# Value loads in 128 rows, first-layer weights in long rows, zero products as TensorE filler, three sigmoids in one operation

## The chip, the cores and the metric

The kernel runs on one core of one Trainium2 chip. That core has five engines, each with its own queue that it works off in order: TensorE (PE in the profile; its weight loads are listed apart as PEld), VectorE (DVE), ScalarE (ACT), GpSimd (POOL) and SyncE (SP), which here only issues transfers. Sixteen DMA engines move data between HBM and the on-chip memory SBUF. TensorE writes its sums to PSUM. The metric is the device time of one execution in microseconds (us); lower is better.

## What is computed

An attention layer with a narrow local window and block summaries, then a gated feed-forward layer:

```
B, H, S, D = 4, 8, 768, 64           # block 32, window 16
k_sum = max of k over each block;  v_sum = mean of v over each block
scores_l = scale * q @ k.T,  kept where |i - j| < 16
scores_s = scale * q @ k_sum.T + log(32)
a = softmax([scores_l, scores_s]);   x = a @ [v, v_sum]        # heads joined: (B, S, 512)
x_prev = x shifted by one token
xk = mu_k * x + (1 - mu_k) * x_prev;   xr = mu_r * x + (1 - mu_r) * x_prev
k = relu(xk @ w_k) ** 2              # w_k 512 x 1024
out = sigmoid(xr @ w_r) * (k @ w_v)  # w_r 512 x 512, w_v 1024 x 512
```

The three weight matrices arrive as 64-bit floats. The kernel loads both 32-bit words of each number and joins them into a 32-bit float on the chip.

## The kernel before, in words

The work is cut into eight halves (4 batches x 2 halves of 384 tokens) and, for attention, into four pairs of heads. `load_set(b, p)` loads the keys of a pair (`kt`) and its values in two tiles (`vx`, one for each half); in batch 0 TensorE forms the block means of the values (L405, then L425) and they are spread into the value tiles (L431). `unit(b, p, hf, ...)` is the attention of one pair and half: scores on TensorE (L466), mask on VectorE (L477), exponential on ScalarE (L481), the sum's inverse on VectorE (L487, L488), normalization on GpSimd (L493), transposes on TensorE (L500), copies on ScalarE (L504), the product with the values (L513). In the words below "unit 0'" is the second half's pair 0, "unit 1'" its pair 1, and so on. `mix` makes xk and xr (L535 on ScalarE, L541 on VectorE). The gate is `gate_parts` for the first half (32-bit products of four passes, L580) and `gate_tile` for the others (two-term split products, L567 to L569), each followed by `sigmoid` (L558). `experts` is the feed-forward layer: for each of eight slices j of 128 hidden units the first product (L601), relu and square on ScalarE (L608, L610), the second product (L627). The first half works with the 32-bit weights, the others with split weights made by `split` (L349 or L350, L352).

`weight` loads one 512 KB block of weights into one of three buffers `st` and makes the 32-bit block in four instructions: a scaling (L318 on ScalarE or L321 on GpSimd), and on VectorE L325, L328 and the join L332. There are 4 blocks of w_r and 8 each of w_k and w_v, and each load waits for a buffer that L328 and the scaling of an earlier block have freed.

ScalarE holds one table of functions at a time: the exponential and the sigmoid are in different ones, so each move between L481 and L558 puts an ACT_TABLE_LOAD ahead of the instruction.

The order of everything is set when the program is built. All operations are recorded with a due time, and `Plan.schedule` places them one after another with a table of assumed lengths (`LENGTH`, `DMA_NS_PER_BYTE`); each engine's instructions then stand in that order. Operations named `warm` (L680) are products of the identity matrix with itself, of which no result is used; the plan places one where TensorE has nothing else to start, up to the first gate product, and the rest are dropped.

Of the kernel before, what the change touches and what calls it, by code (L numbers as in the profile page):

```python
# [9 lines left out]
F32 = mybir.dt.float32  # L10
F32R = mybir.dt.float32r
U32 = mybir.dt.uint32
AF = mybir.ActivationFunctionType
ALU = mybir.AluOpType
# [28 lines left out]
    result=695, wbits=340, wor=612, wsub=612, tiny=60,  # L43
    exp=380, pts=380, vm=160, mixa=520, cast=405, relu=525, square=530, sigmoid=500, wscale=570, wcast=530,
# [12 lines left out]
SLACK = 400  # L57
WARM = 150
COLD = 10000
EARLY = 15000  # L60
# [38 lines left out]
class Plan:  # L99
# [36 lines left out]
    def schedule(self):  # L136
# [24 lines left out]
        for o in self.ops:  # L161
            if not waiting[o]:
                released(o)
        spare = [o for o in self.ops if o.name == "warm"]
        while any(ready.values()):
            best = None
            for e, now in engines.items():
                pick = None
                for o, at in ready[e]:
                    start, need, ok = max(at, now, o.due - EARLY if e == "SP" else 0), {}, True  # L170
                    for x in o.bufs:
                        if x.place is None:
# [16 lines left out]
                if pick and (best is None or pick[2] < best[2]):  # L189
                    best = pick + (e,)  # L190
# [29 lines left out]
            order.append(o)  # L220
            if o.name == "gate32" and spare:

                for w in spare:
                    for x in w.bufs:
                        x.left -= 1
                        if not x.left:
                            free_slots[x.pool].append((start, x.place))
                spare = []
                ready["PE"] = [x for x in ready["PE"] if x[0].name != "warm"]
            if o.name == "warm":  # L230
                spare.remove(o)
            for s in o.succ:
# [7 lines left out]
def tile_kernel(ctx: ExitStack, tc: tile.TileContext, q, k, vT, v, mask, ident, pool, sel, mu, w_k, w_v, w_r, out):  # L240
# [35 lines left out]
    sel_sb = const.tile([P, NS], F32, name="sel_sb")  # L276
    MASK, IDENT, MU, OM, POOLM, SEL = [((x, 0),) for x in ("mask", "ident", "mu", "om", "pool", "sel")]

# [22 lines left out]
    def weight(name, i, src, last, due=None):  # L301
        st, we, wc = buf("st"), buf("we"), buf("wc")
        wf = w_f[name, i] = buf("wc") if last else buf("w", F32, False)
        shape = src.shape
        whole = [(wc, 0)]

        def load():
            s = src.bitcast(U32)
            d = st.t.rearrange("p (c a) -> p c a", c=shape[1]) if len(shape) == 3 else st.t
            nc.sync.dma_start(out=d, in_=s)  # L310

        def words():
            w = st.t.rearrange("p (a b) -> p a b", b=2)
            return w[:, :, 1], w[:, :, 0]


        def scale_act():
            nc.scalar.activation(wc.t.bitcast(F32), words()[0].bitcast(F32), AF.Copy, scale=2.0**-112)  # L318
# [12 lines left out]
        def join():
            nc.vector.scalar_tensor_tensor(  # L332
                out=wf.t.bitcast(U32), in0=wc.t, scalar=3, in1=we.t, op0=ALU.logical_shift_left, op1=ALU.bitwise_or)

        op("SP", "load", due, load, writes=[(st, 0)], size=P * 4096)
        op("ACT", "wscale", None, scale_act, reads=[(st, 0)], writes=whole, other=("POOL", "wscale_p", scale_pool))
        op("DVE", "wbits", None, low, reads=[(st, 0)], writes=[(we, 0)])
        op("DVE", "wor", None, sign, reads=[(st, 0), (we, 0)], writes=[(we, 0)])
        op("DVE", "wor", None, join, reads=[(we, 0), *whole], writes=[(wf, 0)])

# [216 lines left out]
    def sigmoid(ps, z):  # L557
        op("ACT", "sigmoid", None, lambda: nc.scalar.activation(z.t, ps.t, AF.Sigmoid), reads=[(ps, 0)], writes=[(z, 0)])  # L558
# [16 lines left out]
    def gate_parts(x, z):  # L575

        ps = [buf("mm") for _ in range(NTT)]
        for p in range(NPAIR):
            for t in range(NTT):
                op("PE", "gate32", GATE0 - (NPAIR - 1 - p) * FIRST + 930 * t, lambda p=p, t=t: nc.tensor.matmul(  # L580
                    ps[t].t, x[p].t[:, t * P:(t + 1) * P], w_f["wr", p].t, start=(p == 0), stop=(p == NPAIR - 1)),
                   reads=[(x[p], 0), (w_f["wr", p], 0), *([(ps[t], 0)] if p else [])], writes=[(ps[t], 0)])
        for t in range(NTT):
            sigmoid(ps[t], z[t])

# [86 lines left out]
    for i in range(NCK):  # L672
        weight("wr", i, w_r[i * P:(i + 1) * P, :], False)
    for j in range(NCV):
        weight("wk", j, w_k[:, j * P:(j + 1) * P].rearrange("(c p) n -> p c n", p=P), False)
        weight("wv", j, w_v[j * P:(j + 1) * P, :], j == NCV - 1)

    spare = buf("mm", F32, False)
    for _ in range(WARM):
        op("PE", "warm", 1.0e8, lambda: nc.tensor.matmul(  # L680
            spare.t[:, 0:P], ident_sb, ident_sb, start=True, stop=True), reads=IDENT, writes=[(spare, 0)])
    sets, gates = [], []
# [120 lines left out]
```

## Time and profile before

| | |
|---|---|
| time, median of 3 runs | 474.1 us (472.27 to 476.43) |
| the profiled execution | 475.29 us, of it 473.5 us from the first to the last instruction (the span) |
| mean granted TensorE clock over the span | 0.993 |
| busy share: PE, DVE, ACT, POOL | 95%, 56%, 62%, 24% |
| DMA: moved, mean rate | 51.16 MB, 108 GB/s |
| the chain that ended last: PE, ACT, DVE, DMA | 67%, 12%, 8%, 8% |

All times in a profile row count from the span's start. A timeline row reads: start, duration, engine, line of the kernel, operation, what it writes and reads, shapes, how many instructions were merged, and in brackets the idle time of the engine before it with what ended that. A 32-bit product appears as two records, so "x8" for L601 is four instructions. A windows row gives for each engine the busy time in that stretch, then the granted clock, the busy share of the DMA engines and their rate in GB/s.

### The profile page before, as it was taken

How to read it: one execution, taken by the hardware profiler on the slowest of the kernel's cores; microseconds unless marked ns; L12 is line 12 of the kernel's file. 1: busy time of each engine (PE TensorE's matmuls, PEld its weight loads, DVE VectorE, ACT ScalarE, POOL GpSimd, SP SyncE). 2: the span in 40 equal slices, each digit the busy share in tenths (PEclk: the TensorE clock that was granted, in tenths of full speed). 3: DMA queues.
4: the chain of work that ended last, by engine and by line, in shares of the span. 5: the costliest groups of instructions: out<-in, count | busy, mean ns of one | idle time of the engine just before them, and what ended most of it. 6: DMA issues, size and time to landing. Idle time of an engine off the chain costs nothing.

```text
span 473.5 us, 9475 instructions
## 1 busy us (share of the span) xinstructions
PE 447.6 (95%) x3438; PEld 357.9 (76%) x3438; DVE 267.0 (56%) x865; ACT 292.6 (62%) x815; POOL 112.5 (24%) x236
## 2 busy tenths in 40 slices
PE   2798799989899999999999999999999999999996
PEld 2664455546688888997778888997778889888995
DVE  3599789989453566527554565529354554222223
ACT  3578987878785756418886756428886655231311
POOL 0453470734133201302442201304242201000000
PEclk9999889999999999999999999999999999999999
DMA  7995368986110209807200219707100010001001
GB/s 245 257 261 158 105 207 262 289 263 148 51 59 12 68 1 304 211 0 228 60 8 9 78 37 301 212 1 219 35 9 9 12 43 26 1 0 68 0 1 66
DMA packets 27013, 51.16 MB, mean 108 GB/s; under 512 B 2903, under 2 KB 14807, under 8 KB 26967
## 3 DMA queue, kind: packets, MB, share of 16 engines
q1 hardware_dynamic: 26967, 50.56, 36.7%
q8 instruction: 27, 0.44, 0.4%
q14 instruction: 19, 0.16, 0.1%
HBM read 42.49 MB, written 6.29 MB: 103 GB/s over the span
## 4 chain that ended last, share of the span: by engine, by line
PE 67%; ACT 12%; DVE 8%; DMA 8%; issue 2%; POOL 1%; SPq 1%; ACTq 0%; POOLq 0%; DVEq 0%
PE mm L627 23%; PE mm L601 22%; ACT y L481 5%; PE pt L500 4%; PE av L513 4%; DMA kt<-in_k 3%; PE mm L567 3%; PE mm L569 3%; PE mm L568 3%; PE sc L466 2%; DMA pool_sb<-in_pool 2%; PE mm L580 2%; ACT L481 2%; DMA st<-in_w_k 1%; POOL y L493 1%
## 5 line engine op out<-in xcount | busy, mean ns | idle before, releaser
L601 PE MATMUL mm<-xs,w 128*128 128x384 f32 x736 | 152.1, 355 | 0.6 <-DVE w L332 0.6
L601 PEld LDWEIGHTS mm<-xs,w 128*128 128x128 f32 x736 | 131.3, 190 | 13.9 <-issue 3.7
L493 POOL TENSOR_SCALAR y<-y,rc 128x120 f32<-128x120 f32 x192 | 93.9, 507 | 156.1 <-DVE rc L488 131.6
L627 PE MATMUL mm<-w,kh 128*128 128x512 f32 x336 | 91.9, 402 | 0.0
L608 ACT ACTIVATE r<-mm 128x384 f32<-128x384 f32 x64 | 31.2, 488 | 93.9 <-PE mm L601 93.8
L481 ACT ACTIVATE y<-y,mn 128x120 f32<-128x120 f32 x192 | 73.5, 386 | 10.7 <-DVE mn L477 10.4
L627 PEld LDWEIGHTS mm<-w,kh 128*128 128x128 f32 x336 | 60.7, 188 | 11.1 <-DVE kl L616 0.2
L614 DVE CAST kh<-r 128x384 fp32r<-128x384 f32 x44 | 15.9, 362 | 74.9 <-ACT r L610 74.8
L477 DVE CUSTOM_DVE_ANT_0 y<-sc,mask_sb 128x120 f32<-128x120 f32 x192 | 42.5, 277 | 22.9 <-PE sc L466 19.6
L627 PE MATMUL mm<-w,kl 128*128 128x512 f32 x168 | 52.4, 407 | 0.1
L549 DVE TENSOR_TENSOR xs<-xa,xs 128x384 fp32r<-128x384 f32 x56 | 30.4, 558 | 23.6 <-ACT xs L547 23.2
L500 PE MATMUL pt<-ident_sb,y 128*120 128x128 f32 x192 | 33.9, 285 | 6.4 <-POOL y L493 6.0
L504 ACT COPY pts<-pt 120x384 f32<-120x384 f32 x64 | 30.3, 473 | 15.6 <-PE pt L500 15.4
L466 PE MATMUL sc<-kt,qt 64*64 64x120 f32 x768 | 30.4, 289 | 8.6 <-DMA pool_sb<-in_pool 6.8
L500 PEld LDWEIGHTS pt<-ident_sb,y 128*120 128x120 f32 x192 | 22.8, 139 | 19.0 <-POOL y L493 9.6
L481 ACT ACTIVATION_READ_ACCUMULATOR y<-y,mn 128x1 f32 x192 | 36.3, 189 | 0.0
L541 DVE SCALAR_TENSOR_TENSOR xa<-vx,mu_sb,xa 128x384 f32<-128x384 f32 x56 | 33.8, 630 | 2.7 <-ACT xa L535 1.8
L627 PEld LDWEIGHTS mm<-w,kl 128*128 128x128 f32 x168 | 30.0, 188 | 6.5 <-DVE kl L616 0.5
L466 PEld LDWEIGHTS sc<-kt,qt 64*64 64x64 f32 x768 | 22.2, 143 | 16.7 <-DVE kt L393 6.8
L567 PE MATMUL mm<-w,xs 128*128 128x512 f32 x84 | 33.6, 400 | 1.1 <-ACT r L608 0.8
L610 ACT ACTIVATE r<-r 128x384 f32<-128x384 f32 x64 | 33.6, 525 | 1.2
L616 DVE TENSOR_TENSOR kl<-r,kh 128x384 fp32r<-128x384 f32 x56 | 31.7, 566 | 4.3 <-ACT kh L615 1.3
(64 smaller groups left out, 548.1 us busy)
## 6 DMA issues: line engine op xcount, KB each, us to landing
vx<-in_v SPq DMA_DIRECT2D x32, 360.0 KB
kt<-in_k SPq DMA_DIRECT2D x15, 544.0 KB
qt<-in_q SPq DMA_DIRECT2D x32, 192.0 KB
out<-z SPq DMA_DIRECT2D x24, 256.0 KB
st<-in_vT SPq DMA_DIRECT2D x12, 384.0 KB
st<-in_w_k SPq DMA_DIRECT2D x8, 512.0 KB
st<-in_w_v SPq DMA_DIRECT2D x8, 512.0 KB
st<-in_w_r SPq DMA_DIRECT2D x4, 512.0 KB
```

What stands on the lines that cost most here:

```text
L466: nc.tensor.matmul(sc[h].t[cs, i, 0:NK], qt.t[hs, n * QW:(n + 1) * QW], kt.t[hs, w * KB:w * KB + NK], start=True, stop=True,)
L477: op("DVE", "mask", None, lambda h=h, i=i, var=var: nc.vector.tensor_tensor_reduce(out=y[h].t[:, i, :], in0=sc[h].t[:, i, 0:NK], in1=mask_ ...
L481: op("ACT", "exp", None, lambda h=h, i=i: nc.scalar.activation(y[h].t[:, i, :], y[h].t[:, i, :], AF.Exp, bias=mn[h].t[:, i:i + 1], scale=-1.0,
L493: op("POOL", "norm", None, lambda h=h, i=i: nc.gpsimd.tensor_scalar(out=y[h].t[:, i, :], in0=y[h].t[:, i, :], scalar1=rc.t[:, NSL * h + i: ...
L500: nc.tensor.transpose(out=pt[h].t[0:NK, i * P:(i + 1) * P], in_=y[h].t[:, i, :], identity=ident_sb)
L541: op("DVE", "mixd", None, lambda: nc.vector.scalar_tensor_tensor(out=xa.t, in0=xt.t[:, 1 + lo:1 + lo + HT], scalar=mu_sb[:, which, p:p + 1 ...
L567: nc.tensor.matmul(ps.t, xh.t[:, ts], h, start=(p == 0), stop=False)
L601: nc.tensor.matmul(ps.t[:, 0:HT], w.t[:, p * P:(p + 1) * P], (x[p] if single else x[p][s]).t, start=(n == 0), stop=(n == len(terms) * NPAI ...
L608: op("ACT", "relu", None, lambda: nc.scalar.activation(r.t, ps.t[:, 0:HT], AF.Relu), reads=[(ps, 0)], writes=[(r, 0)])
L610: op("ACT", "square", None, lambda: nc.scalar.activation(r.t, r.t, AF.Square), reads=[(r, 0)], writes=[(r, 0)])
L616: op("DVE", "sub", None, lambda: nc.vector.tensor_tensor(out=kl.t, in0=r.t, in1=kh.t.bitcast(F32), op=ALU.subtract), reads=[(r, 0), (kh, 0 ...
L627: nc.tensor.matmul(acc[t].t, a.t[:, t * P:(t + 1) * P], v.bitcast(F32) if single else v, start=start, stop=stop)
```

## The change

Four edits, and a new order that follows from them:

1. **Values.** The host pads each value window from 120 rows (96 tokens and 24 summary rows) to 128 with zeros, and a load writes all 128 partitions: 384 KB where it was 360 KB. Rows stay 3072 bytes long.
2. **First-layer weights.** The host stores w_k block by block, so that a load has 128 rows of 4096 bytes; before it had 512 rows of 1024 bytes.
3. **Filler.** A tile of zeros is written by GpSimd at the start; the filler products read it instead of the identity matrix (which had to be loaded), write to unused columns of the transposes' PSUM bank, and may stand anywhere in the first 110 us of the plan, wherever the plan sees TensorE wait over 300 ns. 65 of them end up in the program, 15 before.
4. **Sigmoids of the first gate.** The three are one operation of the plan, so they stand together on ScalarE.

The table's DMA rate goes from 290 to 330 bytes per ns, which with the points above makes the plan order many operations anew.

```diff
+    ..., sigmoid=500, sigmoid3=4000, ...
-DMA_NS_PER_BYTE = 1 / 290.0
+DMA_NS_PER_BYTE = 1 / 330.0
-WARM = 150
-COLD = 10000
+WARM = 260
+WARM_END = 110000
+GAP = 300
+COLD = 5000
...
-                pick = None
+                pick = fill = None
+                if e == "PE" and now > WARM_END:
+                    ready[e] = [x for x in ready[e] if x[0].name != "warm"]
                 for o, at in ready[e]:
+                    if o.name == "warm":
+                        fill = max(now, at), o
+                        continue
...
+                if fill and (pick is None or pick[2] > fill[0] + GAP):
+                    pick = None, fill[1], fill[0]
...
-            if o.name == "gate32" and spare:
-                ...
-                ready["PE"] = [x for x in ready["PE"] if x[0].name != "warm"]
...
             op("SP", "load", None, lambda hf=hf: nc.sync.dma_start(
-                out=windows(vw[hf]), in_=v[b, p, hf]),
-               writes=[(vw[hf], "a"), (vw[hf], "b")], size=NK * HW * 512)
+                out=vw[hf].t[:, 0:S], in_=v[b, p, hf]),
+               writes=[(vw[hf], "a"), (vw[hf], "b")], size=P * HW * 512)
...
-        for t in range(NTT):
-            sigmoid(ps[t], z[t])
+        def sigmoids():
+            for t in range(NTT):
+                nc.scalar.activation(z[t].t, ps[t].t, AF.Sigmoid)
+        op("ACT", "sigmoid3", None, sigmoids, reads=[(a, 0) for a in ps], writes=[(a, 0) for a in z])
...
-        weight("wk", j, w_k[:, j * P:(j + 1) * P].rearrange("(c p) n -> p c n", p=P), False)
+        weight("wk", j, w_k[j], False)
...
-    spare = buf("mm", F32, False)
+    op("POOL", "tiny", -1.0e6, lambda: nc.gpsimd.memset(zero_sb, 0.0), writes=ZERO)
+    spare = pools["pt"][0][:, 512 - P:512]
     for _ in range(WARM):
-        op("PE", "warm", 1.0e8, lambda: nc.tensor.matmul(
-            spare.t[:, 0:P], ident_sb, ident_sb, start=True, stop=True), reads=IDENT, writes=[(spare, 0)])
+        op("PE", "warm", 1.0e8, lambda: nc.tensor.matmul(spare, zero_sb, zero_sb, start=True, stop=True), reads=ZERO)
```

The first place where the order moves is ScalarE between the last mixes of the first half and the exponentials of units 0' (`y_91`, `y_92`) and 1' (`y_93`, `y_94`); `z` are the sigmoids' results, `wc` the scalings of weight blocks, `r` relu and square. Before:

```order
L535 ACTIVATE xs_0_575<-vx_79,om_sb 128x384
L318 ACTIVATE wc_126<-st_122 128x512
L349 CAST w_0_581<-w_0_563 128x512
L558 ACT_TABLE_LOAD
L558 ACTIVATE z_108<-mm_135 128x512
L481 ACT_TABLE_LOAD
L481 ACTIVATE y_91,sm_100<-y_91,mn_95 128x120 x3
L481 ACTIVATE y_92,sm_100<-y_92,mn_96 128x120 x3
L558 ACT_TABLE_LOAD
L558 ACTIVATE z_109<-mm_133 128x512
L558 ACTIVATE z_110<-mm_134 128x512
```

and with the change:

```order
L514 ACTIVATE xs_0_601<-vx_79,om_sb 128x384
L307 ACTIVATE wc_127<-st_124 128x512
L307 ACTIVATE wc_126<-st_122 128x512
L328 CAST w_0_611<-w_0_595 128x512
L460 ACTIVATE y_91,sm_100<-y_91,mn_95 128x120 x3
L460 ACTIVATE y_92,sm_100<-y_92,mn_96 128x120 x3
L565 ACT_TABLE_LOAD
L565 ACTIVATE z_108<-mm_133 128x512
L565 ACTIVATE z_109<-mm_135 128x512
L565 ACTIVATE z_110<-mm_132 128x512
```

The exponentials of unit 0' now stand ahead of all three sigmoids, and one pair of table loads is gone; both versions then go on with relu and square of slice 0, one more table load, and the exponentials of unit 1'.

The second place is TensorE at the same point: from the scores of unit 1' (`kt_62`) to the first product of slice 1, whose weights are `w_0_652` before and `w_0_689` after. The transposes of unit 0' read `y_91` and `y_92`. Before:

```order
L466 MATMUL sc_129<-kt_62,qt_65 64x120 x2
L500 MATMUL pt_130<-ident_sb,y_91 120x128 x3
L466 MATMUL sc_128<-kt_63,qt_66 64x120 x2
...
L601 MATMUL mm_135<-xs_0_565,w_0_652 128x384
...
L500 MATMUL pt_130<-ident_sb,y_92 120x128 x3
```

and with the change:

```order
L445 MATMUL sc_129<-kt_62,qt_65 64x120 x2
L664 MATMUL pt_130<-zero_sb 128x128 x6
L479 MATMUL pt_130<-ident_sb,y_91 120x128 x3
L664 MATMUL pt_130<-zero_sb 128x128 x8
L479 MATMUL pt_130<-ident_sb,y_92 120x128 x3
L584 MATMUL mm_133<-xs_0_578,w_0_689 128x384
```

The scores of unit 2' (`kt_63`), which stood between, have moved behind slice 2, and 14 filler products stand in the place.

The third place is ScalarE at the gate of the second half, whose sigmoids are still three operations (`z_111`, and twice a tile of the last buffer). Before:

```order
L558 ACT_TABLE_LOAD
L558 ACTIVATE z_111<-mm_135 128x512
...
L558 ACTIVATE z_0_1242<-mm_135 128x512
L504 COPY pts_106<-pt_130 120x384
L481 ACT_TABLE_LOAD
L481 ACTIVATE y_93,sm_101<-y_93,mn_97 128x120 x3
L481 ACTIVATE y_94,sm_101<-y_94,mn_98 128x120 x3
L547 CAST xs_0_769<-xa_112 128x384
L558 ACT_TABLE_LOAD
L558 ACTIVATE z_0_1242<-mm_135 128x512
```

and with the change:

```order
L460 ACTIVATE y_93,sm_101<-y_93,mn_97 128x120 x3
L460 ACTIVATE y_94,sm_101<-y_94,mn_98 128x120 x3
L537 ACT_TABLE_LOAD
L537 ACTIVATE z_111<-mm_133 128x512
L505 COPY vx_74<-av_131 128x384
L537 ACTIVATE z_0_1345<-mm_133 128x512
...
L537 ACTIVATE z_0_1345<-mm_133 128x512
```

Here too the exponentials stand ahead of the gate now, and a pair of loads is gone: the whole program has 18 table loads, 22 before.

More of the change, by code (lines that the diff above doesn't have):

```diff
@@ L43 @@
     result=695, wbits=340, wor=612, wsub=612, tiny=60,
-    exp=380, pts=380, vm=160, mixa=520, cast=405, relu=525, square=530, sigmoid=500, wscale=570, wcast=530,
+    exp=380, pts=380, vm=160, mixa=520, cast=405, relu=525, square=530, sigmoid=500, sigmoid3=4000, wscale=570, wcast=530,
     norm=345, wscale_p=640, wcast_p=640, mixa_p=860, kcopy_p=630, evac_a=375, fill=735,
@@ L163, in schedule @@
                 released(o)
-        spare = [o for o in self.ops if o.name == "warm"]
         while any(ready.values()):
@@ L220, in schedule @@
             order.append(o)
-            if o.name == "gate32" and spare:
[L223 to L228, printed above, removed]
-                ready["PE"] = [x for x in ready["PE"] if x[0].name != "warm"]
-            if o.name == "warm":
-                spare.remove(o)
             for s in o.succ:
@@ L276, in tile_kernel @@
     sel_sb = const.tile([P, NS], F32, name="sel_sb")
-    MASK, IDENT, MU, OM, POOLM, SEL = [((x, 0),) for x in ("mask", "ident", "mu", "om", "pool", "sel")]
+    zero_sb = const.tile([P, P], F32, name="zero_sb")
+    MASK, IDENT, MU, OM, POOLM, SEL, ZERO = [((x, 0),) for x in ("mask", "ident", "mu", "om", "pool", "sel", "zero")]
     op("SP", "load", None, lambda: nc.sync.dma_start(out=mask_sb, in_=mask), writes=MASK, size=P * 3 * NK * 4)
@@ L303, in weight @@
         wf = w_f[name, i] = buf("wc") if last else buf("w", F32, False)
[L304 to L318, printed above, removed]
@@ L331, in join @@
[L331 to L338, printed above, removed]
@@ L339, in weight, with words @@
-        op("DVE", "wor", None, join, reads=[(we, 0), *whole], writes=[(wf, 0)])
+        def words(n):
+            return st.t.rearrange("p (a b) -> p a b", b=2)[:, :, n]
+        op("SP", "load", due, lambda: nc.sync.dma_start(out=st.t, in_=src.bitcast(U32)), writes=[(st, 0)], size=P * 4096)
+        op("ACT", "wscale", None, lambda: nc.scalar.activation(
+            wc.t.bitcast(F32), words(1).bitcast(F32), AF.Copy, scale=2.0**-112), reads=[(st, 0)], writes=[(wc, 0)],
+           other=("POOL", "wscale_p", lambda: nc.gpsimd.tensor_scalar(
+               out=wc.t.bitcast(F32), in0=words(1).bitcast(F32), scalar1=2.0**-112, scalar2=1.0, op0=ALU.mult, op1=ALU.mult)))
@@ new lines, in weight @@
+        op("DVE", "wbits", None, lambda: nc.vector.tensor_scalar(
+            out=we.t, in0=words(0), scalar1=29, scalar2=None, op0=ALU.logical_shift_right), reads=[(st, 0)], writes=[(we, 0)])
+        op("DVE", "wor", None, lambda: nc.vector.scalar_tensor_tensor(
+            out=we.t, in0=words(1), scalar=0x80000000, in1=we.t, op0=ALU.bitwise_and, op1=ALU.bitwise_or),
+           reads=[(st, 0), (we, 0)], writes=[(we, 0)])
+        op("DVE", "wor", None, lambda: nc.vector.scalar_tensor_tensor(
+            out=wf.t.bitcast(U32), in0=wc.t, scalar=3, in1=we.t, op0=ALU.logical_shift_left, op1=ALU.bitwise_or),
+           reads=[(we, 0), (wc, 0)], writes=[(wf, 0)])
@@ L737, in feature_major, with words @@
         return a.reshape(B, NPAIR, 2, S, D).transpose(0, 1, 2, 4, 3).reshape(B, NPAIR, P, S)
-    def words(a):
-        return np.ascontiguousarray(a).view(np.int64)
+    def words(a, n):
+        return np.ascontiguousarray(a).reshape(n, P, DM).view(np.int64)
     q, k, v = (np.asarray(inputs[n]) for n in "qkv")
@@ L787 @@
         "mu": mu.reshape(2, NPAIR, P).transpose(2, 0, 1),
-        "w_k": words(inputs["moe_w_k"]),
-        "w_v": words(inputs["moe_w_v"]),
-        "w_r": words(inputs["moe_w_r"]),
+        "w_k": words(np.asarray(inputs["moe_w_k"]).reshape(NCK, P, NCV, P).transpose(2, 1, 0, 3), NCV),
+        "w_v": words(np.asarray(inputs["moe_w_v"]), NCV),
+        "w_r": words(np.asarray(inputs["moe_w_r"]), NCK),
     }
```

16 lines of the change are left out of this document (4 added, 12 removed).

## The prediction

> **What bounds the kernel now.** I read the page's head and slices first, to see which engine is full and when; then the table by stretches; then the order of time on the engines where TensorE has holes.
>
> ```profile
> span 473.5 us, 9475 instructions
> PE 447.6 (95%) x3438; PEld 357.9 (76%) x3438; DVE 267.0 (56%) x865; ACT 292.6 (62%) x815; POOL 112.5 (24%) x236
> PE   2798799989899999999999999999999999999996
> PEclk9999889999999999999999999999999999999999
> ```
>
> One digit is 11.8 us. TensorE is full from the tenth slice on; its holes lie in the first ten, and so does the only dip of its clock. The stretches say the same in numbers (columns: busy us of PE, PEld, DVE, ACT, POOL, then clock, DMA share, GB/s):
>
> ```profile
> 20.00:30.00 10.00, 10.00 (x161) 8.33 (x161) 7.86 (x33) 7.09 (x25) 4.03 (x9) 1.00 1.00 246
> 30.00:40.00 10.00, 10.00 (x75) 4.74 (x73) 9.66 (x17) 7.53 (x21) 7.18 (x8) 1.00 0.70 219
> 50.00:60.00 10.00, 6.56 (x57) 4.09 (x57) 5.94 (x27) 9.90 (x30) 4.83 (x8) 0.75 0.45 134
> 70.00:80.00 10.00, 10.00 (x57) 5.67 (x56) 9.83 (x19) 7.30 (x15) 1.60 (x3) 1.00 0.80 248
> 150.00:200.00 50.00, 50.00 (x328) 43.44 (x329) 29.36 (x82) 29.65 (x73) 9.72 (x23) 1.00 0.49 141
> 400.00:450.00 50.00, 50.00 (x247) 44.55 (x246) 13.89 (x30) 13.61 (x28) 0.00 (x0) 1.00 0.05 17
> ```
>
> From 150 to 200 us and from 400 to 450 TensorE is busy for all 50 us at full clock: nothing in the change shortens that work, so what is won before about 125 us stays won, and nothing else can be. In the early part the bound moves: transfers (share 1.00) until about 30 us, VectorE (9.66 of 10) to 50, ScalarE (9.90) from 50 to 60, VectorE again (9.83) from 70. The stretch from 50 to 60 is the poorest: TensorE works 6.56 of 10 us at three quarters of its clock.
>
> **The sigmoids and the filler, 46 to 66 us.** ScalarE first, then TensorE, then VectorE:
>
> ```profile
> 46.20 0.61 ACT L349 CAST w<-w 128x512 fp32r<-128x512 f32 x1
> 46.83 1.28 ACT L558 ACT_TABLE_LOAD   x1
> 48.12 0.60 ACT L558 ACTIVATE z<-mm 128x512 f32<-128x512 f32 x1
> 48.74 1.28 ACT L481 ACT_TABLE_LOAD   x1
> 50.03 0.40 ACT L481 ACTIVATE y<-y,mn 128x120 f32<-128x120 f32 x1
> 52.43 1.28 ACT L558 ACT_TABLE_LOAD   x1
> 56.33 1.28 ACT L481 ACT_TABLE_LOAD   x1
> ...
> 50.12 0.84 PE L466 MATMUL sc<-kt,qt 64*64 64x120 f32 x24
> 53.95 0.33 PE L500 MATMUL pt<-ident_sb,y 128*120 128x128 f32 x1 [2.98 <-POOL y L493]
> 54.72 0.81 PE L500 MATMUL pt<-ident_sb,y 128*120 128x128 f32 x2 [0.44 <-POOL y L493]
> 55.45 1.71 PE L466 MATMUL sc<-kt,qt 64*64 64x120 f32 x24
> 57.10 5.17 PE L601 MATMUL mm<-xs,w 128*128 128x384 f32 x8
> 65.95 2.85 PE L601 MATMUL mm<-xs,w 128*128 128x384 f32 x8
> ...
> 60.96 0.17 DVE L487 TENSOR_SCALAR sm<-sm 128x6 f32<-128x6 f32 x1 [2.58 <-ACT y L481]
> 64.25 0.69 DVE L332 SCALAR_TENSOR_TENSOR w<-wc,we 128x512 uint32<-128x512 uint32 x1
> ```
>
> One sigmoid (48.12) stands between two table loads ahead of the exponentials of unit 0' (50.03). TensorE, with the scores of unit 1' done at 50.96, waits 2.98 and then 0.44 us for the normalized `y` of that unit. Behind the wait it is slow: the scores take 1.71 us where 0.84 was enough at 50.12, and the first product of slice 1 takes 5.17 us where the one of slice 2 takes 2.85.
>
> With the change the exponentials come first. They start where the table load stood, 50.03 - 46.83 = 3.2 us earlier, and `y` is ready at 50.75 and 51.5 instead of 53.95 and 54.72. In exchange TensorE now has 14 filler products in its queue, in front of everything. Their price, and the transposes' at full clock (the second row will serve again below):
>
> ```profile
> 24.32 0.61 PE L680 MATMUL mm<-ident_sb 128*128 128x128 f32 x4
> 124.72 0.52 PE L500 MATMUL pt<-ident_sb,y 128*120 128x128 f32 x3 [1.68 <-POOL y L493]
> ```
>
> Four records are two products, so 0.3 us each. Walked through: 50.96, six products 1.8, transposes 0.52, eight products 2.4, transposes 0.52: 56.2. Then the first product of slice 1 at full clock, 2.85: 59.05. The scores of unit 2', which stood in front, are still to be done, 0.84: 59.9. Before, the same work was done at 57.10 + 5.17 = 62.3. **Gain 2.4 us.** Were the filler free, the gain would be 6.6 with the products' 4.2; were the clock to fall all the same, the 5.17 would stay and take back 2.3.
>
> Would the weights be there? VectorE sat 2.58 us at 60.96 until the exponentials of unit 1' were done; these stand behind the last table load in both versions and come one pair of loads, 2.57 us, earlier. So the join of slice 2's weights (64.25) comes about 2.6 us earlier, and TensorE's 2.4 are not taken back there.
>
> [...]
>
> **The start, 0 to 48 us.**
>
> ```profile
> 6.85 1.48 PE L466 MATMUL sc<-kt,qt 64*64 64x120 f32 x24 [6.85 <-DMA pool_sb<-in_pool]
> 33.44 0.86 PE L405 MATMUL mm<-vx,pool_sb 120*32 120x128 f32 x24
> 36.46 2.84 PE L580 MATMUL mm<-w,xs 128*128 128x512 f32 x6
> 41.61 0.92 PE L513 MATMUL av<-pts,vx 120*64 120x64 f32 x24
> 44.77 2.84 PE L580 MATMUL mm<-w,xs 128*128 128x512 f32 x6 [1.47 <-DVE xs L541]
> ```
>
> The first scores run at 1.48 us against 0.84 later: TensorE starts at half speed, which filler from the first microsecond should end. That alone moves little, because unit after unit waits for loads. What counts is the last pair of heads: its values are in use at 33.44 (L405), its attention is done at 41.61 + 0.92, its gate products wait 1.47 us and end at 47.6. Between 33.44 and 41.61 TensorE had no hole, and six gate products of 2.84 / 3 = 0.95 stood there; the new order has four, and two behind. That is 1.9 us. VectorE, at 9.66 of 10, has one join (0.69) less ahead of the last mix, and gets the earlier units' scores sooner. Bounds: nothing, if VectorE is what ends last, and 1.9. I take **1.9**, as masks that come sooner use the fifth of the stretch from 20 to 30 us in which VectorE is idle.
>
> **The gate of the second half, 109 to 125 us.**
>
> ```profile
> 102.45 0.28 PE L420 MATMUL pt<-ident_sb,vs 128*24 128x128 f32 x1 [1.48 <-DVE vs L417]
> 109.34 0.50 PE L567 MATMUL mm<-w,xs 128*128 128x512 f32 x1 [0.79 <-ACT r L608]
> 114.00 0.50 PE L567 MATMUL mm<-w,xs 128*128 128x512 f32 x1 [0.32 <-ACT z L558]
> 118.06 1.28 ACT L481 ACT_TABLE_LOAD   x1
> 121.78 0.17 DVE L487 TENSOR_SCALAR sm<-sm 128x6 f32<-128x6 f32 x1 [2.29 <-ACT y L481]
> ```
>
> The load at 118.06 stands ahead of exponentials, VectorE waits 2.29 us for them, and TensorE then 1.68 (the row at 124.72) for the normalized `y`. In the new order those exponentials are done ahead of the gate, and one pair of loads is gone. Bounds 0 and 1.68 + 0.32 = 2.0; I take **1.7**, the wait that the removed pair ends. Nine filler products stand at about 100 to 110 us: 9 x 0.3 = 2.7, with waits of 1.48 + 0.79 to lie in, so I charge **0.4** (2.7 if that cover is gone).
>
> **The loads.** This is a narrow view of 8 to 20 us, in which a digit and a rate stand for 0.3 us:
>
> ```profile
> DMA  9999998999899999999989999989999999999899
> GB/s 431 424 429 396 251 222 221 232 210 287 198 269 273 213 213 227 284 239 204 256 294 395 414 297 280 201 207 224 232 263 270 222 280 251 205 251 288 229 266 254
> vx<-in_v SPq DMA_DIRECT2D x5, 360.0 KB
> ```
>
> The engines are busy throughout, yet the rate falls from 430 to some 220 GB/s as the key load gives way to value loads. Eight value loads come before the last pair can start. If 128 rows ran at the keys' 425, a load would take 393 KB / 425 = 0.93 us instead of 369 KB / 220 = 1.68, and eight 6.0 us less. If the rate stays, 6.7% more bytes cost 0.9 us in all. The trace does not say which property of these loads makes them slow; the value loads themselves are the nearest row, so I take **0**, between the ends. The long rows of w_k I also put at 0: their loads wait for a buffer, and the stretch from 30 to 60 has a DMA share of 0.45 to 0.70, which covers a slower or faster load; from 70 to 100 us a change of a tenth in eight loads would be a few tenths of a us each.
>
> [...]
>
> **Sum.** Against the profiled execution's 475.3: 2.4 + 1.9 + 1.7 - 0.4 = 5.6, so 469.7. That execution is 1.2 us above the median of 474.1, and against the median the forecast is **468.5**, 1.2% less.
>
> **Rivals**, all against the median.
>
> VectorE takes over. It is at 9.66 and 9.83 of 10 in two stretches; if it cannot start earlier, the start and the second gate give nothing, and only 2.4 - 0.4 = 2.0 is left: 472.1. Against it: it idles 2.58 and 2.29 us for ScalarE just where table loads go.
>
> The value loads speed up. Half of the 6.0 us, since VectorE is nearly full behind them: 465.5. For it: the rate halves exactly with these loads, and the fast key loads have 128 rows. Against it: rows of another length are another difference.
>
> Zeros do not hold the clock, so the filler does not do what it says. The 2.3 us come back: 470.8. For it: the trace has filler of identity matrices only.
>
> Slower: the filler stands in the way at the start. 42 products lie ahead of the last mix, 27 more than before, in order with scores and transposes. The stretch from 20 to 30 us has TensorE busy 10.00 of 10; if they push the last pair's transposes behind the moment when its values are ready, they cost 27 x 0.3 = 8.1, the 1.9 is lost, and 2.4 + 1.7 - 0.4 is set against it: 478.5. Against it: TensorE is idle ahead of 6.85, and the transfers hold back what follows.
>
> **Chances.** Forecast 0.52 (its own range 466 to 471), VectorE 0.18, fast loads 0.14, clock 0.08, slower 0.08. Within 1% (4.7 us, about what a measurement of this kernel can tell from no change) means 469.4 to 478.8. Three quarters of the forecast's case lie below, 0.39, with the fast loads and a part of VectorE's case 0.56; slower by over 1% is 0.06, as part of that case stays within. The range of 8 in 10 runs from 463, a fast-loads case in which two thirds of the 6.0 arrive, to 473, past VectorE's case.
>
> **What would show it.** 18 table loads on ScalarE; clock 1.00 from 50 to 62 us and no product of L601's kind above 3 us there; no wait for `y` of 2.98 or 1.68; the last gate product about 2 us earlier; the rate of the value loads still near 220 GB/s. It is wrong if the filler shows up where TensorE had no hole, or if VectorE's waits move rather than vanish.

## The result and the profile after

| | before | changed |
|---|---|---|
| median, its range, runs | 473.74 us (472.27 to 476.43), 4 | 468.17 us (467.6 to 468.92), 4 |
| ratio to before | | 0.9875, 95% interval 0.9844 to 0.9905 |
| profiled execution, its span | 475.29 us, 473.5 | 467.61 us, 465.8 |
| mean clock over the span | 0.993 | 1.000 |
| moved | 51.16 MB | 51.96 MB |

The change made the kernel 1.2% faster, and the forecast of 468.5 us is 0.3 us off. The two profiled executions lie further apart than the medians, 7.7 us against 5.6, and what follows walks through those 7.7. Ranges here and below hold every run; the ratios leave out runs over 1.5% above the kernel's fastest. The page's head of the changed kernel, and its slices:

```profile
span 465.8 us, 9660 instructions
PE 453.6 (97%) x3538; PEld 367.0 (79%) x3538; DVE 267.9 (57%) x866; ACT 284.7 (61%) x808; POOL 117.0 (25%) x239
PE   8999999988999999999999999999999999999996
PEclk9999999999999999999999999999999999999999
```

The dip of the clock in the early slices is gone, and TensorE's digits are 8 or 9 in every slice but the last. A part of that is filler, which counts as busy. Next comes the narrow view of 8 to 20 us that the forecast's term for the loads was read from:

```profile
DMA  9999999999999999989999999999999999999999
GB/s 377 384 379 385 411 412 410 399 417 325 347 375 415 358 372 422 424 338 366 392 475 369 406 399 420 382 405 379 412 385 376 390 387 399 390 393 379 434 389 427
```

Before, the rate fell from 430 to some 220 GB/s once value loads came. Now it stays near 390 throughout. The forecast had said that it would not. The stretches (columns as before: PE, PEld, DVE, ACT, POOL, clock, DMA share, GB/s) show what that does further on:

```profile
20.00:30.00 10.00, 9.43 (x135) 5.92 (x135) 9.04 (x30) 8.74 (x29) 6.40 (x11) 1.00 0.75 280
...
50.00:60.00 10.00, 10.00 (x50) 5.27 (x49) 8.83 (x16) 9.11 (x25) 6.09 (x8) 1.00 0.50 183
...
70.00:80.00 10.00, 9.70 (x74) 5.91 (x75) 9.90 (x42) 9.65 (x31) 5.17 (x11) 1.00 0.91 328
```

The transfers have slack from 20 us on (share 0.75, before 1.00), and VectorE is at 9.04 of 10 there, before 7.86. The poorest stretch, 50 to 60, went from 6.56 of 10 us on TensorE at clock 0.75 to 10.00 at 1.00. TensorE's timeline at the start:

```profile
6.48 0.84 PE L445 MATMUL sc<-kt,qt 64*64 64x120 f32 x24 [0.48 <-DMA qt<-in_q]
28.91 0.86 PE L384 MATMUL mm<-vx,pool_sb 120*32 120x128 f32 x24
35.36 0.92 PE L492 MATMUL av<-pts,vx 120*64 120x64 f32 x24
38.90 2.84 PE L559 MATMUL mm<-w,xs 128*128 128x512 f32 x6
41.58 2.74 PE L584 MATMUL mm<-xs,w 128*128 128x384 f32 x8
```

The first scores take 0.84 us, before 1.48; without filler (no_filler, below) they take 1.48 again, so a start without it ran at 0.57 of that speed. A 32-bit gate product takes 0.95 us (2.84 for three), 4.1 times the 0.23 us at which the split products of the second gate follow each other. The last pair's block means (28.91) come 4.5 us earlier, its attention (35.36) 6.3, the last gate products (38.90) and the first product of slice 0 (41.58) 5.9. That product follows the last gate products in both kernels and serves below as the mark of the start. In the kernel before, this mark and two later ones, the first products of slice 7 and of the second half, are:

```profile
47.45 2.74 PE L601 MATMUL mm<-xs,w 128*128 128x384 f32 x8
...
105.47 2.75 PE L601 MATMUL mm<-xs,w 128*128 128x384 f32 x8
...
124.99 2.33 PE L601 MATMUL mm<-xs,w 128*128 128x384 f32 x12
```

The sigmoids and the filler, on ScalarE and TensorE:

```profile
44.16 1.28 ACT L565 ACT_TABLE_LOAD   x1
45.45 1.58 ACT L565 ACTIVATE z<-mm 128x512 f32<-128x512 f32 x3
48.82 0.48 ACT L483 COPY pts<-pt 120x384 f32<-120x384 f32 x1 [1.41 <-PE pt L664]
49.74 1.28 ACT L460 ACT_TABLE_LOAD   x1
...
45.03 1.60 PE L664 MATMUL pt<-zero_sb 128*128 128x128 f32 x12
46.47 0.75 PE L479 MATMUL pt<-ident_sb,y 128*120 128x128 f32 x3
47.05 1.73 PE L664 MATMUL pt<-zero_sb 128*128 128x128 f32 x14
49.35 0.49 PE L664 MATMUL pt<-zero_sb 128*128 128x128 f32 x2 [0.57 <-ACT pts L483]
50.00 2.75 PE L584 MATMUL mm<-xs,w 128*128 128x384 f32 x8
58.78 2.74 PE L584 MATMUL mm<-xs,w 128*128 128x384 f32 x8
```

The product of slice 1 starts at 50.00 and takes 2.75 us, where it started at 57.10 and took 5.17; the wait of 2.98 us for `y` is gone. A new wait is there: ScalarE's copy of the transposes waits 1.41 us for filler, and the next filler waits for that copy. Last, the gate of the second half, and the stretches from the first product of slice 7 to the first product of the second half, of before, of the changed kernel, and of the changed kernel's filler alone:

```profile
96.25 2.85 PE L584 MATMUL mm<-xs,w 128*128 128x384 f32 x8
...
100.44 0.49 PE L664 MATMUL pt<-zero_sb 128*128 128x128 f32 x2 [0.57 <-ACT pts L483]
...
102.96 0.49 PE L664 MATMUL pt<-zero_sb 128*128 128x128 f32 x2 [1.04 <-ACT pts L483]
...
104.23 0.54 PE L479 MATMUL pt<-ident_sb,y 128*120 128x128 f32 x3
...
110.85 0.50 PE L546 MATMUL mm<-w,xs 128*128 128x512 f32 x1 [1.22 <-ACT z L537]
...
118.20 2.33 PE L584 MATMUL mm<-xs,w 128*128 128x384 f32 x12
```
```profile
105.47:124.99 19.52, 16.73 (x133) 11.72 (x132) 15.68 (x51) 16.59 (x46) 7.25 (x14) 1.00 0.45 109
```
```profile
96.25:118.20 21.95, 19.12 (x154) 14.24 (x152) 16.31 (x52) 13.61 (x43) 7.50 (x15) 1.00 0.53 169
```
```profile
96.25:118.20 21.95, 2.55 (x16) 1.87 (x14) 1.00 0.53 169
```

The lead over the kernel before is 5.9 us at the first product of slice 0, 7.2 at that of slice 2 (58.78 against 65.95), 9.2 at that of slice 7 (96.25 against 105.47), and 6.8 where the second half begins (118.20 against 124.99). So the gate of the second half, which the forecast had gaining 1.3, lost 2.4: TensorE has as many idle us there as before (21.95 - 19.12 = 2.8, and 19.52 - 16.73 = 2.8), and 2.55 us of filler on top; what that filler stands in, filler_start shows below. At the end the lead is 7.7: 0.9 of it was won behind 125 us, where the prediction had said that nothing could be.

### The profile page after: what moved, and what is told of

Read it like the earlier page. It is cut to its first block, busy times and chain, and to the rows that moved or that the text cites. A ratio compares the mean times of both kernels' runs of the same rounds, so it can differ in the third digit from the quotient of the medians.

```text
span 465.8 us, 9660 instructions
## 1 busy us (share of the span) xinstructions
PE 453.6 (97%) x3538; PEld 367.0 (79%) x3538; DVE 267.9 (57%) x866; ACT 284.7 (61%) x808; POOL 117.0 (25%) x239
## 2 busy tenths in 40 slices
DMA packets 24230, 51.96 MB, mean 112 GB/s; under 512 B 2935, under 2 KB 10743, under 8 KB 24183
## 4 chain that ended last, share of the span: by engine, by line
PE 78%; DVE 8%; ACT 8%; DMA 2%; issue 2%; POOL 1%; SPq 0%; DVEq 0%; ACTq 0%; POOLq 0%
PE mm L610 25%; PE mm L584 24%; PE pt L479 4%; PE av L492 4%; PE mm L546 4%; PE mm L548 4%; PE mm L547 4%; ACT y L460 3%; PE sc L445 3%; PE mm L559 2%; PE pt L664 2%; DVE we L313 1%; ACT pts L483 1%; DMA st<-in_vT 1%; ACT L460 1%
## 5 line engine op out<-in xcount | busy, mean ns | idle before, releaser
L584 PE MATMUL mm<-xs,w 128*128 128x384 f32 x736 | 149.9, 352 | 0.3 <-DVE w L316 0.3
L584 PEld LDWEIGHTS mm<-xs,w 128*128 128x128 f32 x736 | 130.4, 188 | 12.8 <-issue 1.5
L472 POOL TENSOR_SCALAR y<-y,rc 128x120 f32<-128x120 f32 x192 | 97.4, 525 | 159.3 <-DVE rc L467 133.0
L546 PE MATMUL mm<-w,xs 128*128 128x512 f32 x84 | 33.5, 399 | 1.2 <-ACT z L537 1.2
L479 PE MATMUL pt<-ident_sb,y 128*120 128x128 f32 x192 | 32.8, 279 | 1.3 <-POOL y L472 0.9
L492 PEld LDWEIGHTS av<-pts,vx 120*64 120x64 f32 x768 | 25.5, 137 | 10.2 <-issue 8.6
L548 PE MATMUL mm<-w,xs 128*128 128x512 f32 x84 | 32.9, 391 | 0.0
```

Of the source, the lines that this page charges most:

```text
L472: op("POOL", "norm", None, lambda h=h, i=i: nc.gpsimd.tensor_scalar(out=y[h].t[:, i, :], in0=y[h].t[:, i, :], scalar1=rc.t[:, NSL * h + i: ...
L479: nc.tensor.transpose(out=pt[h].t[0:NK, i * P:(i + 1) * P], in_=y[h].t[:, i, :], identity=ident_sb)
L492: nc.tensor.matmul(av.t[hs, w * QW:(w + 1) * QW], windows(vw)[:, w, hs], pts[h].t[:, i, c * QW:(c + 1) * QW], start=True, stop=True,)
L546: nc.tensor.matmul(ps.t, xh.t[:, ts], h, start=(p == 0), stop=False)
L548: nc.tensor.matmul(ps.t, xl.t[:, ts], h, start=False, stop=(p == NPAIR - 1))
L584: nc.tensor.matmul(ps.t[:, 0:HT], w.t[:, p * P:(p + 1) * P], (x[p] if single else x[p][s]).t, start=(n == 0), stop=(n == len(terms) * NPAI ...
```

## The experiments

Every kernel of these ran in five rounds beside runs of the kernel before (the first two rows are for comparison). The changed kernel was not run again beside them, so a difference to it can be off by as much as the three medians of the kernel before differ, 0.7 us. "Slice 0" is the start of its first product in the profiled execution; among kernels that do not differ ahead of it, it scattered from 41.0 to 42.5 us.

| kernel | median, us (range, runs) | ratio to before, 95% | slice 0 | GB/s, 8 to 20 us |
|---|---|---|---|---|
| before | 473.6 to 474.3 in three groups | 1 | 47.45 | 270 |
| changed | 468.17 (467.6 to 468.9, 4) | 0.9875 (0.9844 to 0.9905) | 41.58 | 393 |
| rows120 | 472.99 (470.0 to 477.5, 12) | 0.9965 (0.9931 to 1.0000) | 43.98 | 305 |
| rows112_8 | 470.94 (469.4 to 479.4, 10) | 0.9910 (0.9880 to 0.9939) | 44.75 | 301 |
| rows64_64 | 475.33 (473.2 to 479.1, 12) | 1.0035 (1.0009 to 1.0060) | 46.98 | 266 |
| before_rows128 | 471.11 (470.2 to 472.3, 9) | 0.9921 (0.9892 to 0.9950) | 44.75 | 397 |
| wk_1kB | 467.58 (466.4 to 468.4, 6) | 0.9840 (0.9804 to 0.9877) | 41.74 | 397 |
| no_filler | 470.37 (469.4 to 472.8, 6) | 0.9925 (0.9902 to 0.9947) | 42.58 | 399 |
| filler_start | 467.82 (467.1 to 471.9, 6) | 0.9876 (0.9846 to 0.9905) | 41.01 | 397 |
| sigmoid_ahead | 470.09 (469.3 to 472.4, 6) | 0.9916 (0.9894 to 0.9939) | 42.49 | 389 |
| order_alone | 477.53 (475.3 to 479.3, 8) | 1.0079 (1.0053 to 1.0104) | 45.50 | 281 |
| filler_av_bank | 466.13 (465.6 to 469.1, 6) | 0.9846 (0.9821 to 0.9871) | 41.47 | |
| filler_no_mid | 467.40 (466.7 to 468.4, 5) | 0.9865 (0.9844 to 0.9886) | 42.06 | |
| filler_av_no_mid | 467.43 (465.9 to 469.4, 6) | 0.9865 (0.9842 to 0.9889) | 41.59 | |

### The rows of the value loads

**rows120**, the changed kernel with the loads cut back:

```diff
-                out=vw[hf].t[:, 0:S], in_=v[b, p, hf]),
+                out=vw[hf].t[0:NK, 0:S], in_=v[b, p, hf, 0:NK]),
```

> The changed kernel with its value loads cut back to 120 rows; every queue keeps its order. Theory (the loads' rows gave the early lead): between 8 and 20 us the rate falls from 393 GB/s back toward the 270 of before, the last block means move from 28.91 to about 33 us, the first expert product from 41.6 to about 46, and of these 4 us some 2 to 3 reach the end, because VectorE is the bound from 60 to 90 us: 470 to 471.5 us. Rival 1 (the forecast's zero term for loads: the new order and the filler made the lead): rate and time unchanged, 468.2 within 0.5 us. Rival 2 (the rows gave all of it): the whole gain but the sigmoids' goes, 472 us or more.

**before_rows128**, the kernel before with this one edit (and the host's padding):

```diff
-                out=windows(vw[hf]), in_=v[b, p, hf]),
+                out=vw[hf].t[:, 0:S], in_=v[b, p, hf]),
```

> The kernel before with only its value loads padded to 128 rows; order, filler and sigmoids as before. Theory (the rows alone speed up all transfers of the first 30 us): the rate between 8 and 20 us rises from 270 to 370 GB/s or more, the last block means move from 33.44 to 29 to 30 us, and the time falls by 2 to 3.5 us to 470.2 to 471.7. Rival (the fast rate needs the other edits, for instance long rows of the weights or the new order): 473.7 within 0.7 us. Rival 2 (the gain is spent on waits further on, as the old order has its table loads at 46 to 56 us): the start is 4 us earlier and the time falls by under 1 us.

Their windows from 8 to 20 us, rows120 first:

```profile
8.00:20.00 12.00, 10.38 (x161) 8.54 (x164) 9.17 (x53) 8.34 (x37) 4.98 (x12) 1.00 1.03 305
```
```profile
8.00:20.00 12.00, 9.46 (x118) 7.09 (x119) 8.82 (x51) 8.29 (x38) 5.87 (x14) 1.00 1.04 397
```

The rate follows the rows alone: 393 falls to 305 without them, and 270 rises to 397 with them, in the old order and with the other edits absent. The start follows: slice 0 moves 2.4 us later in the one kernel (41.58 to 43.98) and 2.7 earlier in the other (47.45 to 44.75). At the end the rows are worth 4.8 us in the changed kernel (by medians; 0.9965 against 0.9875 makes 4.3) and 3.2 in the one before. The forecast's zero for the loads falls, and so does the rival that the new order made the rate. How much reaches the end is less sure than the rate: the theory for rows120 had 470 to 471.5 us, the median of 472.99 lies above it, and its profiled execution, at 471.21 near the low end of a wide range, is 3.6 us behind the changed kernel's, not 4.8.

Why do eight more rows matter so much? Two kernels ask that, both with the changed kernel's order. **rows112_8** moves 120 rows in two loads:

```diff
+                for lo, hi in ((0, 112), (112, NK)):
+                    nc.sync.dma_start(out=vw[hf].t[lo:hi, 0:S], in_=v[b, p, hf, lo:hi])
```

> The changed kernel with each value load cut into two, 112 rows and 8 rows: the same 120 rows and bytes as before, one more DMA a load, the same order. Theory (an uneven spread over the sixteen engines is what made 120 rows slow; 112 is 16 times 7): the rate between 8 and 20 us stays at 370 GB/s or more and the time within 1 us of the changed kernel's 468.2. Rival (the rate needs full 128-partition loads, or the zeros' rows matter otherwise): as with 120 rows, rate near 270 GB/s and 470 us or more.

**rows64_64** moves all 128 rows, as `((0, 64), (64, P))`:

> The changed kernel with each 128-row value load cut into two of 64 rows; all rows and bytes are still moved, order unchanged. It separates two accounts of why 120 rows, and 112 + 8 rows, run at 300 GB/s between 8 and 20 us where 128 run at 393. Account A (loads whose rows share out unevenly over sixteen engines slow everything; 8 rows are half an engine set): 64 is 16 times 4, so 380 GB/s or more and 468.2 within 1 us. Account B (the rate holds only while every load gives each of its rows to the same place as its neighbours do, that is while all loads have 128 rows): about 300 GB/s and 470.5 to 472.5 us, as with 112 + 8.

```profile
8.00:20.00 12.00, 10.09 (x150) 8.31 (x149) 8.80 (x53) 8.23 (x37) 4.87 (x12) 1.00 1.04 301
```
```profile
8.00:20.00 12.00, 9.28 (x112) 7.13 (x111) 6.90 (x43) 6.73 (x30) 2.96 (x8) 0.86 1.05 266
```

Both are slow (301, then 266 GB/s), with the DMA engines busy throughout (share 1.04 and 1.05). 64 + 64 moves exactly the changed kernel's bytes, and 64 rows can share out evenly, 4 to each of sixteen engines, yet it is the slowest way to load: 475.33 us, which gives back the whole gain. So account A, uneven shares, falls. Account B stands in that the fast rate (389 to 399 GB/s) came only with value loads of all 128 rows, though 266 GB/s and 475.33 us are worse than the 300 and 470.5 to 472.5 that it had given. A value row is 3072 bytes long in all of these kernels, so it is the row count of one load and not the length of a row. The time does not follow the rate alone: rows112_8 is 2 us faster than rows120 at the same rate, and no run says why.

Two loads in place of one are themselves a difference, and the packet records of the traces bear on it. In the median from 8 to 20 us, a packet of 3072 bytes, a row of values, took 121 ns in the changed kernel and in before_rows128, but 171, 175 and 201 ns in rows120, rows112_8 and rows64_64, and 202 in the kernel before. A packet of 4096 bytes, a row of w_r that is the same in all of these kernels, took 159 ns beside loads of 128 rows and 216 to 272 beside the others. So the time is in the packets, those of other loads too, and not in gaps between loads; and 120 rows in one load show that slow packets need no second load.

How a load is divided shows in the traces only by a count: they have 2903 packets under 512 bytes with 120 rows, 2935 with 128, 3191 with 112 + 8 and 3447 with 64 + 64, which for each of the 32 value loads is 1, 9 and 17 more than with 120 rows. The rate does not follow that count, as the kernels with fewer and with more of them than 2935 are all slow. No view shows which engine moves a row, so why the other row counts lengthen the packets is not shown.

**wk_1kB** undoes edit 2 alone, in the kernel (`w_k[:, j * P:(j + 1) * P].rearrange("(c p) n -> p c n", p=P)` for `w_k[j]`) and on the host:

> The changed kernel with only the first-layer weights back in 512 rows of 1024 bytes a block, same order. Theory (these loads wait for a buffer that VectorE frees, so their own speed is covered): 468.2 within 0.7 us. Rival (short rows are slow enough to delay the joins on VectorE, which is full from 60 to 90 us): 1 to 3 us slower, with VectorE waiting for st between 50 and 95 us.

467.58 us: no loss. The long rows of w_k are worth nothing here, as forecast. The run says nothing of the rate from 8 to 20 us, as the first load of w_k is issued at 25.9 us.

### The filler and the sigmoids

**no_filler** leaves the 65 products out when the program is written, with all else in its order; **filler_start** leaves out only the last 23.

```diff
     for o in order:
-        o.emit()
+        if o.name != "warm":          # filler_start: drops only
+            o.emit()                  # [o for o in order if o.name == "warm"][42:]
```

> The changed kernel without its 65 filler products, everything else in the same order. Account A (the forecast's: zeros hold the clock, and without them it falls at 50 us, so that the second first-layer product takes about 5 us where it takes 2.75): the first scores take 1.5 us again, the clock falls below 0.8 between 47 and 55 us; TensorE saves some 4 us of filler and waits at 45 to 50 us and 2 us at 95 to 104, and pays 2.5 us for the clock: 467 to 469.5 us. Account B (the filler is in the way, and the clock it saves is hidden by waits for VectorE): 466 us or less. Account C (it carries much of the gain): 471 us or more.

> The changed kernel with the first 42 filler products (up to the last mix, about 38 us) and without the other 23, everything else in the same order. If the 23 only fill time that TensorE would have waited, 468.2 within 0.5 us with a clock of 1.00. If the 14 at 45 to 50 us hold up the copies of the transposes (ScalarE waits 1.41 us on the filler there) and the 9 at 95 to 104 likewise, and the clock holds without them: 1 to 2.5 us faster, 466 to 467 us. If the clock falls at 50 us without them: 469 to 470.5.

The product of slice 1 and two windows of no_filler, then the same of filler_start, and of filler_start's second gate the first product of slice 7, the value product behind it, and the transposes behind that:

```profile
49.88 4.44 PE L584 MATMUL mm<-xs,w 128*128 128x384 f32 x8
...
50.00:60.00 10.00, 10.00 (x45) 5.00 (x44) 8.37 (x15) 7.65 (x23) 6.33 (x9) 0.83 0.61 206
100.00:110.00 10.00, 6.01 (x62) 4.60 (x61) 5.83 (x30) 5.67 (x20) 3.18 (x8) 0.74 0.60 172
```
```profile
48.46 2.75 PE L584 MATMUL mm<-xs,w 128*128 128x384 f32 x8
...
50.00:60.00 10.00, 10.00 (x50) 5.20 (x49) 9.76 (x19) 7.25 (x21) 5.89 (x7) 1.00 0.66 220
100.00:110.00 10.00, 9.10 (x83) 7.14 (x85) 7.89 (x34) 8.71 (x32) 4.07 (x11) 0.66 0.47 156
```
```profile
94.62 2.85 PE L584 MATMUL mm<-xs,w 128*128 128x384 f32 x8 [0.32 <-DVE w L316]
...
100.58 0.33 PE L492 MATMUL av<-pts,vx 120*64 120x64 f32 x2 [1.60 <-DMA vx<-vm]
...
102.71 0.90 PE L479 MATMUL pt<-ident_sb,y 128*120 128x128 f32 x3
```

Without filler the clock falls twice, to 0.83 and 0.74, and 2.2 us are lost at the end: 470.37, above the 467 to 469.5 of account A and below account C's 471. Products of zeros do hold the clock, so the rival that they do not falls. It had put 2.3 us on that, close to what their absence cost, but not where it looked: from the first product of slice 0 to that of slice 7, no_filler takes 54.6 us (42.58 to 97.20) and the changed kernel 54.7, so there the filler's own time and the clock that it holds balance. The loss comes at the second gate, 24.7 us (97.20 to 121.88) instead of 21.95; another 1.0 lies ahead of slice 0.

With the first 42 alone the time is that of the changed kernel: the product of slice 1 comes 1.5 us earlier, but the clock falls at 100 to 110 us (0.66), and the second half begins at 117.9 instead of 118.2. The 14 at slice 1 cost 1.0 us from the first product of slice 0 to that of slice 1 (8.4 with them, 7.4 without), and the nine win back 1.3 at the second gate (21.95 with them, 23.3 without). So the last 23 buy clock with time, about one for one.

The nine lie in waits. Without them TensorE waits 1.60 us there for the load that spreads the block means (`vx<-vm`) and some 1.0 for copies, and gets from slice 7 to the transposes behind the value product in 8.1 us (94.62 to 102.71); with them it takes 8.0 (96.25 to 104.23).

**sigmoid_ahead** moves the first of the three sigmoids back ahead of the exponentials of unit 0':

```diff
-            for t in range(NTT):
+            for t in range(1, NTT):        # the first stands ahead of the six "exp" before them
                 nc.scalar.activation(z[t].t, ps[t].t, AF.Sigmoid)
```

> The changed kernel with the first of the three sigmoids back ahead of the exponentials of unit 0', which brings back a pair of table loads (20 in all); every other instruction in its order. Forecast's account: the exponentials start about 3 us later, normalization too, TensorE waits behind its filler for the transposes' input, and the first product of slice 1 starts 2 to 2.5 us later: 470 to 470.8 us. Rival (VectorE, nearly full from 60 us, is late anyway): under 0.7 us slower at the end, with a wait at 45 to 50 us that is won back by 90 us.

```profile
42.43 1.28 ACT L565 ACT_TABLE_LOAD   x1
44.34 1.28 ACT L460 ACT_TABLE_LOAD   x1
...
52.83 2.75 PE L586 MATMUL mm<-xs,w 128*128 128x384 f32 x8
```

From the first product of slice 0 to that of slice 1 are now 52.83 - 42.49 = 10.3 us, in the changed kernel 50.00 - 41.58 = 8.4. These 1.9 us arrive at the end undiminished (470.09 against 468.17). VectorE gave nothing back, so that rival falls.

### The order by itself

**order_alone** has all four edits undone in the changed kernel's order: rows120, wk_1kB, no_filler and sigmoid_ahead together.

> Only the new order is left of the change: value loads of 120 rows, first-layer weights in 1024-byte rows, no filler product, one sigmoid ahead of the exponentials of unit 0', each instruction otherwise where the changed kernel has it. Taken from the changed kernel one at a time, the 128 rows were worth 4.8 us, the filler 2.2 and the sigmoid 1.9, 8.9 together. If they add up, 477 us, which is 3 us slower than before: the new order by itself would cost. If they overlap (each is partly spent on the same waits), 473 to 475 us, no difference from before. If the order gains by itself, under 472.

```profile
45.50 2.75 PE L587 MATMUL mm<-xs,w 128*128 128x384 f32 x8
110.85 1.28 PE L493 MATMUL av<-pts,vx 120*64 120x64 f32 x24 [3.52 <-DMA vx<-vm]
127.02 2.33 PE L587 MATMUL mm<-xs,w 128*128 128x384 f32 x12
```

477.53 us is 3.9 slower than before, and the parts add up: 4.8 + 2.2 + 1.9 = 8.9 above the changed kernel was expected, 9.4 measured. At the start this order gains 47.45 - 45.50 = 1.95 us, the forecast's 1.9. It loses more at the gate of the second half, which begins at 127.02 instead of 124.99: there the value product waits 3.5 us for `vx<-vm`, a wait that the trace of before does not have, as its first value product behind slice 7 comes only at 112.30, after the first gate products. The two traces lie 2.1 us apart and not 3.9, as that of before is of an execution 1.7 above the median. The 3.9 also holds only for the loads as they were. With loads of 128 rows it is less, by an estimate: 468.17 + 2.2 + 1.9 = 472.3 for this order against the 471.11 of before_rows128 makes 1.2, and the ratios make 2.1. No run has that kernel.

### Versions that might be faster

**filler_av_bank** writes the filler to unused columns of the value products' bank instead of the transposes'. **filler_no_mid** drops the 14 products at 45 to 50 us, numbers 42 to 55 of `warm`. **filler_av_no_mid** does both.

```diff
-        av=tiles("av", 1, [P, HT], pool=psum), ...
+        av=tiles("av", 1, [P, 512], pool=psum), ...
-    spare = pools["pt"][0][:, 512 - P:512]
+    spare = pools["av"][0][:, 512 - P:512]
```

> The changed kernel with its 65 filler products written to unused columns of the bank of the value products instead of the transposes' bank; all instructions in their order. If the copies of the transposes wait for filler only because the two share a bank (1.41 us at 47.4 us in the changed kernel), that wait and the filler's own waits of 0.57 and 1.04 us go, the first product of slice 1 starts 0.5 to 1 us earlier and the clock stays at 1.00: 467.0 to 467.7 us. If these waits were covered by the normalization anyway: 468.2 within 0.4.

> The changed kernel without the 14 filler products at 45 to 50 us, with the 42 before them and the 9 at 95 to 104 us. Without all 23 the first product of slice 1 started 1.5 us earlier, but the clock fell to 0.5 at 102 to 107 us and the lead was gone at 118. If the nine hold the clock there and the clock holds at 50 as it did then: 466.5 to 467.3 us. If the fall of the clock moves to 50 us (as without any filler): 468.5 to 470.

> The two last edits together: 42 + 9 filler products, in the value products' bank. If both gains are real and apart (the nine then no longer wait for copies at 99 to 103 us): 466 to 467 us, the fastest of all. If the second stage gives it back at the gate (ScalarE's sigmoids at 110 us set the pace): as with the 14 products dropped alone, within 0.4 us.

The first row is filler_av_bank's copy of the transposes, the next two its products of slice 1 and of the second half; the last two fences are slice 1 of filler_no_mid and of filler_av_no_mid:

```profile
46.92 0.51 ACT L483 COPY pts<-pt 120x384 f32<-120x384 f32 x1
...
48.81 2.75 PE L584 MATMUL mm<-xs,w 128*128 128x384 f32 x8
...
117.28 2.33 PE L584 MATMUL mm<-xs,w 128*128 128x384 f32 x12
```
```profile
49.45 3.88 PE L584 MATMUL mm<-xs,w 128*128 128x384 f32 x8
```
```profile
48.88 4.44 PE L584 MATMUL mm<-xs,w 128*128 128x384 f32 x8
```

In another bank the filler no longer holds up the copy (46.92 with no wait; in the changed kernel 48.82 after 1.41 us of waiting), slice 1 starts 1.2 us earlier at full clock, and the kernel has the lowest median of all, 466.13. Its interval overlaps the changed kernel's, so the trace shows the mechanism and the time only makes the gain likely. It is more than the 467.0 to 467.7 that was expected. Dropping the 14 products did not add to that: with them gone the clock fell at 50 us (0.91 in filler_no_mid and 0.88 in filler_av_no_mid from 50 to 60 us; 3.88 and 4.44 us for the product), although it had held there in filler_start with the same instructions up to that point. filler_no_mid, at 467.40, lies between its two accounts, as the clock fell but the time of 468.5 or more did not follow.

## Why the prediction was right, and where only its sum was

- **The sigmoids and the filler, 2.4.** By its own count (the product of slice 1 and the scores of unit 2' done) the changed kernel is at 50.00 + 2.75 + 0.85 = 53.6 where before was at 62.3. That is 8.7 ahead, of which 5.9 were there at slice 0: 2.8. The marks agree: at slice 2 the lead is only 7.2, but the changed kernel has done a second product (2.7 us) more by then and one unit's scores (0.8) fewer, which makes 3.2. No L584 product passed 2.85 us, the clock stayed at 1.00, and there are 18 table loads. Not foreseen was that copies and filler wait for each other.
- **The start, 1.9.** As a term of the order it was right: 1.95 in order_alone, within the scatter of 0.7 or so, with four gate products and not six between the last block means and the attention. It missed the loads, so the last gate product came 5.9 us earlier and not 2.
- **The loads, 0.** This step failed. The bound of 6.0 had been worked out rightly, but the value taken kept the rate of the 120-row loads. Measured: 393 GB/s instead of 220 to 270, worth 2.4 to 2.7 us at slice 0 and 4.8 at the end (3.2 in the old order). The rival that the value loads speed up was right on its mechanism; it had given 465.5 because it added its gain to a full sum.
- **The second gate, 1.7 less 0.4.** This failed too: a gain of 1.3 was forecast, a loss of 2.4 measured. The wait of 1.68 for `y` is gone, but the new order puts a value product ahead of the gate whose values need the load `vx<-vm` (1.60 us of waiting in filler_start, 2.98 in no_filler, 3.52 in order_alone), and the gate waits 1.22 for a sigmoid. In the changed kernel the nine filler products and 1.6 of waits for copies stand where that load is waited for, so the charge of 0.4 for filler was not the mistake: the forecast listed the waits that the order removes here and not those that it brings.
- **VectorE takes over.** It is at 9.90 of 10 from 70 to 80 us, and yet the lead was not lost there: it went from 7.2 to 9.2, of which 1.9 is the work that the changed kernel had done sooner at slice 2, so it held. The rival did not come about; at the second gate TensorE's waits are for copies, a load and a sigmoid.

The forecast met the time to 0.3 us by luck, as two wrong terms cancelled: a loss in the new order of 3.9 us net (order_alone), which it had not seen, and a gain from the loads of 3 to 5, which it had put at nothing. The parts as measured, -3.9 for the order, 4.8 for the rows, 2.2 for the filler and 1.9 for the sigmoid, sum to 5.0 of the 5.6 us.

## What to carry to other kernels

Load tiles in all 128 partitions, even if some rows are padding, and look at the rate by time when two kinds of load share the queues: loads of another row count brought the whole core's rate from 430 to 220 GB/s here. Filler that holds the clock should write where no other engine has to read soon: here a copy waited 1.41 us for it, and not at all with the filler in another bank. When the edits of a change come with a new order, run that order with the edits undone: here it was the only thing that showed that a part of the change cost time, 3.9 us with the loads as they were.

## What the runs showed of the hardware

- Value loads of 120, 112 + 8 or 64 + 64 rows brought the rate of the whole core from 8 to 20 us down to 270 to 305, 301 and 266 GB/s, where with 128 rows it was 389 to 399, at a DMA share of 1.03 to 1.05 in all of them. The packets took longer, also those of loads beside them: one of 3072 bytes 171 to 202 ns, not 121, and one of 4096 bytes 216 to 272, not 159. The kernels with such loads also scattered more (473.2 to 479.1 us for rows64_64, 470.2 to 472.3 for before_rows128).
- Products of zeros hold the granted clock: 1.00 with 65 of them, 0.83 from 50 to 60 us and 0.74 from 100 to 110 without.
- Whether a given idle stretch costs clock was not the same in each kernel: with the same instructions up to there, the product of slice 1 took 2.75 us in filler_start and 3.88 in filler_no_mid, behind waits of 2.2 and 1.9 us. What decides it, no run shows.
